# Block-causal attention and a gated unit: a written instruction order replaced by another, with staging rings of five instead of six and the last output tile in two halves

## The chip, the cores and the metric

The kernel runs on one core of a Trainium2 chip. The metric is the device time of the whole program in microseconds (us), as the median of several runs. All engine names are those of the profile: PE is TensorE (matmuls), PEld its weight loads, DVE is VectorE, ACT is ScalarE, POOL is GpSimd, and SP is SyncE, whose queue issues nearly all the transfers.

## The reference

Attention with a block mask (a query sees its own block of 64 keys and all before it), then a gated unit whose gate is a causal convolution of five taps:

```python
B, H, S, D = 8, 8, 576, 64
scores = q @ k.T / sqrt(D)
scores = where(block(i) >= block(j), scores, -1e9)      # block = position // 64
attn = softmax(scores)
x = (attn @ v).transpose(0, 2, 1, 3).reshape(B, S, 512)  # heads side by side

gate_pre = sum(conv_w[k] * x_shifted_by(4 - k) for k in range(5))
gate = sigmoid(gate_pre)
out = (gate * (x @ w_val)) @ w_out                       # float32, [8, 576, 512]
```

The inputs are float32; q, k and v are drawn at a tenth of a normal draw.

## The kernel before, in words

**Order.** Nothing is scheduled by a compiler. The whole program is one long string of *words* (`PLAN`, line 20 on), and `run` executes them one by one: each word calls a function that issues the instructions of one step. Each engine works off its own instructions strictly in the order in which the words stand, so the string fixes the order on every engine and in SP's queue of transfers at once. A word carries numbers and, behind an `@`, either the PSUM banks that it writes (`@45`: banks 4 and 5; there are eight) or the engine that does it (`@A` ACT, `@D` DVE, `@P` POOL).

**Attention.** A "couple" a = 0 to 15 is four heads' worth of q or k, 576 rows of 64. For it `Lqk.a.0` and `Lqk.a.1` load q and k (576 KB each) into the ring `qks`; `cq` casts each to fp16; `tq` transposes it on DVE; `kz` copies the two end blocks of k into a small padded tile. `s.a.t...` computes the transposed scores of key tiles t = 0, 1, 2. The array's four strips of 32 rows work on four heads at once: rows 0 and 1 are half r = 0, rows 2 and 3 are half r = 1. A word such as `s.0.0.0.0.2.1@0123` computes two halves side by side (couple 0, t = 0, r = 0 and couple 0, t = 2, r = 1), `s.2.0@2367` both halves of one t, and a word with three numbers, such as `s.3.2.0@01`, one half alone. `e.a.t.r` takes the exponential of one half on ACT, reading its two banks and writing `pt`. There are 96 of them. `m.p` masks the pair p = 2a + r on POOL (a copy and two memsets). `Lv.p`, `cv.p`, `Lvt`, `cvt` load v (two transfers of 128 KB each) and cast it on POOL with a column of ones. `av.p.h` multiplies probabilities and v for one head (15 small matmuls), `n.p.h` normalises on DVE (a reciprocal and a multiplication), then `xtr.p` transposes on PE and `xt.p` evacuates on DVE, or `xd.p` does both by a transposing transfer in SP's queue (10 of the 32 pairs).

**Gated unit.** When a batch of four pairs stands in `xt`, `cn.n` runs the convolution (80 matmuls of 32 x 32 tiles, into four banks), `th.n.r` takes the tanh on ACT, `val.n.x` projects with `w_val` (four matmuls), `gv.n.x` multiplies the two on DVE, `o.n.t` projects with `w_out` (four matmuls), `oc.n.t` evacuates to `osb` and `st.n.t` stores. n = 0 to 7 are the batches' first 512 rows; n = 8 and 9 collect the last 64 rows of four batches each. `DG` on POOL builds the taps' diagonal tiles, which `cn.0` is the first to need; `wv`, `wo`, `wp`, `wq` prepare the weights.

**Fillers.** `w@b` is one 128 x 128 x 512 matmul on zeros into bank b; nothing reads it. There are 19 of them.

**Rings.** The line `NQS, NVS, ... = 6, 6, 3, 2, 4, 7, 4, 3, 2, 5` sets how many staging buffers q/k (`qks`), v (`vst`) and the rest have. A load into a ring waits until the cast of what lay there is done, and whatever stands behind it in SP's queue waits too. `osb` has five buffers for the output tiles, which take turns in the order of `TILES`.

**The first couple.** `START` and the words `cqr`, `tqr` bring in k and q of couple 0 in parts: k in two parts of 10 and 8 of its 18 column groups, q in three of 4, 6 and 8, each part cast in two pieces by ACT, DVE and POOL.

**The end.** Batch 7's last row tile is written in two halves of 256 columns (`o.7.3`, `o.7.4`); tile `o.9.1` is the last one of all and is written whole. `store` sends a tile of n = 8 or 9 as two transfers of 64 rows.

Of the kernel before, what the change touches and what calls it, by code (L numbers as in the profile page):

```python
# [15 lines left out]
w@0 w@0 Lqk.1.0 w@0 Lqk.1.1 w@0 w@0 Lqk.2.1 w@0 Lcn w@0 Lvt.0 w@0 w@0 Lv.0 cqr.1.1.0@A cqr.1.0.1@D  # L16
cqr.1.1.1@P cqr.1.0.0@A tqr.1.1 tqr.1.0 cqr.0.1.0@A cqr.0.2.1@P cqr.0.2.0@D cqr.0.0.0@P kz.0@A
cqr.0.1.1@P tqr.0.2 cqr.0.0.1@P tqr.0.0 tqr.0.1 s.0.0.0.0.2.1@0123 Lqk.2.0 cq.1.0@P
s.0.2.0.0.1.1@4567 e.0.0.0 tq.1.0 Lv.1 cq.1.1@P e.0.1.1 w@0 w@0 e.0.2.0 w@0 tq.1.1 cq.2.1@P
s.0.0.1.0.1.0@0167 e.0.2.1 Lqk.3.0 kz.1@D Lv.3 s.1.2.0@45 e.0.1.0 cvt.0 tq.2.1 cv.0 w@2 e.1.2.0 cw@2  # L20
m.0 kz.2@D e.0.0.1 Lqk.3.1 s.1.0@6745 cq.2.0@P cT Lv.2 av.0.0@2 e.1.0.0 av.0.1@3 n.0.0 cv.1
s.1.1.0@01 e.1.0.1 s.1.1.1@67 n.0.1 m.1 tq.2.0 e.1.1.1 s.1.2.1@23 Lwv.1 cq.3.0@P Lv.5 av.1.1@4
e.1.2.1 av.1.0@5 n.1.1 xtr.0@6 cv.3 e.1.1.0 s.2.0.1@23 xt.0 m.3 n.1.0 s.2.1.1@67 e.2.0.1 s.2.1.0@01
tq.3.0 Lvt.1 m.2 s.2.2.1@45 e.2.1.1 Lwv.0 av.3.0@2 cq.3.1@P Lv.4 av.3.1@3 e.2.2.1 s.2.0.0@67 n.3.1
cv.2 e.2.1.0 n.3.0 s.2.2.0@45 m.5 av.2.1@3 tq.3.1 Lqk.4.0 e.2.2.0 av.2.0@2 Lqk.4.1 DG@P n.2.1
e.2.0.0 Lv.6 s.3.2.0@01 kz.3@D xtr.1@3 n.2.0 e.3.2.0 cvt.1 s.3.0.0.3.1.1@4567 xt.1 cv.5 xtr.3@2
e.3.1.1 s.3.2.1@01 m.4 Lwo.1 xt.3 wv.2@D av.5.0@3 Lwo.0 e.3.0.0 av.5.1@2 cv.4 Lv.7 n.5.0 w@6 e.3.2.1
s.3.1.0.3.0.1@6745 wv.3@D xtr.2@3 n.5.1 e.3.0.1 cq.4.0@P w@0 av.4.0@0 xt.2 xtr.5@1 wv.1@A wv.0@D
cn.0@4523 e.3.1.0 Lqk.5.0 xt.5 cq.4.1@P tq.4.0 Lqk.5.1 av.4.1@1 th.0.0 Lvt.2 val.0.2@6 n.4.0 m.6
th.0.1 tq.4.1 val.0.3@0 cv.6 Lv.8 wo.1@A gv.0.2 kz.4@P s.4.1.1.4.2.0@4523 n.4.1 av.6.0@6 e.4.1.1  # L30
wo.0@P gv.0.3 val.0.0@7 n.6.0 e.4.2.0 m.7 Lqk.6.1 wp@1045 val.0.1@6 wq.2@A wq.0@D cv.7 wq.3@A gv.0.0
av.6.1@2 wq.1@A Lv.9 av.7.0@3 gv.0.1 cq.5.0@P s.4.1.0.4.0.1@0145 n.6.1 n.7.0 av.7.1@6 e.4.0.1
o.0.0@7 cq.5.1@P n.7.1 Lqk.6.0 e.4.1.0 tq.5.0 s.4.2.1.4.0.0@2345 Lv.11 cvt.2 o.0.2@6 e.4.0.0
oc.0.0@D cv.8 xtr.4@0 tq.5.1 e.4.2.1 xtr.6@1 m.8 o.0.3@7 Lqk.7.1 xt.4 m.9 s.5.2.0.5.1.1@4523 xt.6
oc.0.3@D av.8.0@0 e.5.2.0 kz.5@P o.0.1@1 oc.0.2@D cv.9 e.5.1.1 n.8.0 cq.6.1@P st.0.2
s.5.1.0.5.0.1@6745 oc.0.1@D Lv.10 av.9.0@0 e.5.0.1 xtr.7@1 cq.6.0@P n.9.0 w@2 Lqk.7.0 s.5.2.1@23
e.5.1.0 s.5.0.0@45 xt.7 Lv.13 tq.6.1 cv.11 av.9.1@0 e.5.2.1 w@1 av.8.1@1 tq.6.0 Lqk.8.1 e.5.0.0
cn.1@2367 m.11 n.8.1 cq.7.1@P Lqk.9.0 n.9.1 val.1.2@4 th.1.0 Lqk.8.0 kz.6@D val.1.3@5 m.10 th.1.1
tq.7.1 s.6.1.0.6.2.1@0123 cv.10 st.0.0 gv.1.3 val.1.1@6 e.6.1.0 Lvt.3 kz.7@P gv.1.2 cq.7.0@P
Lqk.10.1 av.10.0@7 e.6.2.1 gv.1.1 s.6.1.1.6.2.0@4501 Lv.14 n.10.0 xtr.9@6 e.6.2.0 xt.9 av.11.0@2  # L40
av.11.1@3 tq.7.0 e.6.1.1 w@0 s.6.0.0@67 n.11.0 s.7.0@0145 Lqk.9.1 e.6.0.0 n.11.1 av.10.1@2 e.7.0.0
xtr.8@3 m.12 xtr.11@6 xt.8 val.1.0@7 Lv.12 e.7.0.1 n.10.1 cq.8.1@P xt.11 s.7.1.0@01 s.6.0.1@23
gv.1.0 s.7.2.0@45 e.7.1.0 cq.8.0@P xtr.10@6 o.1.3@7 xt.10 e.6.0.1 tq.8.1 val.2.0@6 cv.13 Lqk.11.0
e.7.2.0 m.13 oc.1.3@D Lv.15 s.7.2.1@01 tq.8.0 cn.2@4523 cvt.3 e.7.2.1 cq.9.0@P s.8.2.1@01 th.2.0
Lvt.5 o.1.1@7 Lqk.10.0 m.14 kz.8@A gv.2.0 th.2.1 Lv.16 val.2.1@4 oc.1.1@D cq.9.1@P e.8.2.1 av.13.1@5
gv.2.1 s.8.2.0.8.0.1@2367 n.13.1 cv.12 o.1.0@0 e.8.0.1 st.0.1 cv.14 st.1.1 s.7.1.1@45 cv.15 e.8.2.0
s.8.1.0@67 Lvt.4 tq.9.0 val.2.2@1 st.0.3 e.7.1.1 av.12.1@2 tq.9.1 e.8.1.0 Lv.17 val.2.3@3 m.15
n.12.1 oc.1.0@A s.8.0.0.8.1.1@4567 cq.10.1@P Lqk.11.1 kz.9@A gv.2.3 av.12.0@0 e.8.0.0 Lv.19 gv.2.2
av.13.0@2 cq.10.0@P n.12.0 av.14.1@3 e.8.1.1 av.14.0@1 n.13.0 w@0 cq.11.0@P n.14.0
s.9.1.1.9.2.0@4567 xtr.12@2 n.14.1 e.9.2.0 av.15.1@0 xt.12 m.17 av.15.0@1 n.15.1 e.9.1.1  # L50
s.9.0.1.9.1.0@2367 m.16 n.15.0 o.1.2@0 e.9.0.1 tq.10.1 cvt.4 xtr.14@1 e.9.1.0 xtr.13@4 cv.16 o.2.2@5
# [36 lines left out]
"""


@with_exitstack
def kernel(
    ctx: ExitStack,
    tc: tile.TileContext,
# [8 lines left out]
    nc = tc.nc  # L103
# [5 lines left out]
    B, H, SEQ, D = q.shape  # L109
# [389 lines left out]
```

## Time and profile before

| | |
|---|---|
| runs | 171.86 us (median of three: 171.4, 171.86, 173.29) |
| the profiled execution | 170.84 us, of which the span from the first to the last instruction is 169.1 us |
| PE, PEld | busy 158.1 and 99.8 us, 3117 instructions each |
| ACT | busy 128.5 us; the 96 exponentials take 92.1 us of it |
| DVE | busy 124.0 us |
| POOL | busy 100.5 us; 30 full casts of q or k take 42.0 us |
| transfers | 41.97 MB, 248 GB/s on average |

A busy PE in this table says that a matmul was in flight, not that the array did as much as it can: matmuls overlap, and their ends are modelled. To see how full PE is, the starts of consecutive matmuls are compared. The "chain" of a profile is the work that ended last, followed back from the end: at each step to what released it, or to the instruction before it on its engine.

### The profile page before, as it was taken

How to read it: one execution, taken by the hardware profiler on the slowest of the kernel's cores; microseconds unless marked ns; L12 is line 12 of the kernel's file. 1: busy time of each engine (PE TensorE's matmuls, PEld its weight loads, DVE VectorE, ACT ScalarE, POOL GpSimd, SP SyncE). 2: the span in 40 equal slices, each digit the busy share in tenths (PEclk: the TensorE clock that was granted, in tenths of full speed). 3: DMA queues.
4: the chain of work that ended last, by engine and by line, in shares of the span. 5: the costliest groups of instructions: out<-in, count | busy, mean ns of one | idle time of the engine just before them, and what ended most of it. 6: DMA issues, size and time to landing. Idle time of an engine off the chain costs nothing.

```text
span 169.1 us, 7342 instructions
## 1 busy us (share of the span) xinstructions
PE 158.1 (94%) x3117; PEld 99.8 (59%) x3117; DVE 124.0 (73%) x264; ACT 128.5 (76%) x158; POOL 100.5 (59%) x193
## 2 busy tenths in 40 slices
PE   7299989899999999999999999999999999999980
PEld 2047776646675865577665676665647568454640
DVE  3775988999999976699897489568897638542640
ACT  5479999798797998998858898978578983537230
POOL 5688999959688299789495449454993424000000
PEclk9999999999999999999999999999999999999996
DMA  5999979999569999993589499999989687853665
GB/s 191 400 357 355 312 203 342 364 363 325 184 153 309 372 359 276 317 294 98 145 214 373 117 289 172 238 357 161 357 237 254 131 152 107 174 189 124 224 217 125
DMA packets 55867, 41.97 MB, mean 248 GB/s; under 512 B 45973, under 2 KB 46229, under 8 KB 55834
## 3 DMA queue, kind: packets, MB, share of 16 engines
q1 hardware_dynamic: 55690, 41.37, 85.2%
q8 instruction: 24, 0.39, 1.0%
q10 hardware_dynamic: 144, 0.13, 0.2%
q14 instruction: 9, 0.07, 0.1%
HBM read 30.42 MB, written 9.44 MB: 236 GB/s over the span
## 4 chain that ended last, share of the span: by engine, by line
PE 81%; ACT 6%; DVE 6%; DMA 2%; issue 1%; POOL 0%; DVEq 0%
PE B L113 78%; ACT pt L279 6%; PE B L316 4%; DMA qks<-in_k_dram 2%; DVE kT L240 2%; DVE qT L240 2%; DVE x L309 1%; DVE rc L308 0%; ACT w_val L230 0%; POOL qk L224 0%; ACT osb L224 0%; DVE xt L329 0%; DVE qk L224 0%; DVEq L308 0%; DVEq L240 0%
## 5 line engine op out<-in xcount | busy, mean ns | idle before, releaser
L279 ACT ACTIVATE pt<-B 128x1024 f16<-128x1024 f32 x96 | 92.1, 1034 | 13.8 <-PE B L113 13.1
L224 POOL CAST qk<-qks 128x1152 f16<-128x1152 f32 (+2 forms) x35 | 43.8, 1268 | 14.8 <-DMA qks<-in_k_dram 6.1
L113 PE MATMUL B<-qT,kT 32*128 32x448 f16 (+3 forms) x640 | 35.1, 296 | 4.0 <-DVE qT L240 3.2
L113 PEld LDWEIGHTS <-pt 128*128 128x128 f16 x960 | 33.1, 98 | 5.9 <-issue 1.1
L113 PE MATMUL B<-xt,w_val 128*128 128x512 f16 (+1 forms) x160 | 36.0, 359 | 0.0
L113 PE MATMUL B<-w_out,gv 128*128 128x512 f16 (+1 forms) x148 | 35.8, 374 | 0.0
L113 PE MATMUL B<-v,pt 128*128 128x65 f16 x896 | 35.1, 194 | 0.0
L309 DVE TENSOR_TENSOR x<-B,rc 128x320 f16<-128x320 f32 x64 | 31.5, 492 | 2.3
L385 DVE SCALAR_TENSOR_TENSOR gv<-th,B 128x512 f16<-128x512 f32 (+1 forms) x40 | 24.1, 628 | 12.3 <-ACT th L373 8.9
L113 PEld LDWEIGHTS <-kT 32*128 32x128 f16 x640 | 19.0, 95 | 20.8 <-issue 11.8
L373 ACT ACTIVATE th<-B 128x1024 f32<-128x1024 f32 (+1 forms) x20 | 18.1, 939 | 10.6 <-PE B L113 10.6
L113 PEld LDWEIGHTS <-w_val 128*128 128x128 f16 x160 | 14.0, 98 | 12.5 <-issue 1.1
L218 POOL CAST v<-vst 128x512 f16<-128x512 f32 x32 | 19.5, 618 | 3.2 <-PE B L113 1.9
L240 DVE STREAM_TRANSPOSE qT<-qk 128x576 f32<-128x576 f32 (+3 forms) x18 | 19.4, 1107 | 2.4 <-PE B L113 1.6
L308 DVE RECIPROCAL rc<-B 128x5 f32<-128x5 f32 x64 | 11.8, 185 | 11.7 <-PE B L113 11.6
L240 DVE STREAM_TRANSPOSE kT<-qk 128x576 f32<-128x576 f32 (+2 forms) x17 | 19.5, 1153 | 1.3 <-POOL qk L224 0.7
L287 POOL MEMSET pt<- 64x384 f16 x32 | 13.2, 412 | 11.1 <-ACT pt L279 9.7
L113 PEld LDWEIGHTS <-gv 128*128 128x128 f16 x148 | 13.0, 98 | 11.5 <-issue 0.6
L224 ACT COPY osb<-B 128x512 f32<-128x512 f32 (+1 forms) x21 | 11.8, 582 | 9.1 <-PE B L113 4.8
L286 POOL COPY pt<-pt 128x128 f16<-128x128 f16 x32 | 9.6, 300 | 8.7 <-ACT pt L279 8.3
L113 PE MATMUL B<-xt,DG 32*32 32x512 f16 (+1 forms) x800 | 13.3, 357 | 0.1
L113 PE MATMUL B<-v16t,pt 128*128 128x65 f16 x64 | 12.4, 194 | 0.0
(46 smaller groups left out, 109.3 us busy)
## 6 DMA issues: line engine op xcount, KB each, us to landing
qks<-in_k_dram SPq DMA_DIRECT2D x16, 576.0 KB, 6.6
qks<-in_q_dram SPq DMA_DIRECT2D x16, 576.0 KB, 5.3
vst<-in_v_dram SPq DMA_DIRECT2D x64, 128.0 KB, 5.2
out_dram<-osb SPq DMA_DIRECT2D x31, 256.0 KB, 3.4
out_dram<-osb SPq DMA_DIRECT2D x9, 128.0 KB, 2.8
vtst<-in_v_dram SPq DMA_DIRECT2D x8, 128.0 KB, 6.6
th<-in_moe_w_val_dram SPq DMA_DIRECT2D x2, 512.0 KB, 7.1
osb<-in_moe_w_out_dram SPq DMA_DIRECT2D x2, 512.0 KB, 7.1
```

The source lines that it names most:

```text
L113: nc.tensor.matmul(out=out, lhsT=lhsT, rhs=rhs, start=start, stop=stop, skip_group_check=True)
L218: nc.gpsimd.tensor_copy(out=v16s[p % NV][0:128, 0:4, 0:2, 0:64], in_=vst[p % NVS][0:128])
L224: (eng.copy if eng is nc.scalar else eng.tensor_copy)(out=o, in_=i)
L240: nc.vector.transpose(out=(qT, kT)[i][a % NQT][0:128].bitcast(fp32).rearrange("p c (x n) -> p c n x", n=9)[:, :, x // 2:y // 2], in_=qk16[ ...
L279: nc.scalar.activation(out=pts[(2 * a + r) % NPT][0:128, 0:2, 512 * t:512 * t + 512], in_=two(bank["s", a, t, 2 * r], bank["s", a, t, 2 * ...
L286: nc.gpsimd.tensor_copy(out=pt[0:128, 0:2, 1536:1600], in_=pt[0:128, 0:2, 0:64])
L287: nc.gpsimd.memset(pt[64:128, 0:2, 0:1536].rearrange("p h (t s) -> p h t s", t=3)[:, :, :, 0:64], 0.0)
L308: nc.vector.reciprocal(out=rc[0:128], in_=O[:, :, 64:65])
L309: nc.vector.tensor_tensor(out=x16[p % NX16][0:128, 0:5, h, 0:64], in0=O[:, :, 0:64], in1=rc[0:128].to_broadcast([128, 5, 64]), op=ALU.mult)
L316: nc.tensor.transpose(out=f16(m[0])[:, 128 * i:128 * i + 128], in_=x16[p % NX16][0:128, i, 0:2, 0:64], identity=ident16[0:128, 0:128])
L373: nc.scalar.activation(out=ths[ORDER.index(n) % NTH][0:128, 2 * r:2 * r + 2, 0:w], in_=two(bank["cn", n, 2 * r], bank["cn", n, 2 * r + 1], w),
L385: nc.vector.scalar_tensor_tensor(out=gvs[z % NG][0:128, x, 0:w], in0=ths[z % NTH][0:128, x, 0:w], scalar=1.0, in1=f32(bank["val", n, x])[: ...
```

## The change

The string `PLAN` is replaced as a whole: 832 words before, 833 after. The same steps are in it, with the same 19 fillers and the same 10 transposing transfers; their order, their banks and, for some, their engine differ. Beside that, `NQS` and `NVS` go from 6 to 5, and the last tile of n = 9 is written in two halves: `o.9.1` and `o.9.2` instead of `o.9.1`, the second of the halves' two transfers on ACT's queue.

By count of words: scores as 59 words instead of 61 (halves that stand alone: 22 instead of 26); 38 `o`, `st` instead of 37; `cq.1.0` on DVE, all other full casts on POOL as before; `kz` on ACT, DVE, POOL 2, 6, 8 times instead of 6, 4, 6; `oc` 24 times on ACT and 14 on DVE instead of 21 and 16; of the casts of the first couple four on ACT, two on DVE, four on POOL instead of 3, 2, 5; `wv` 2 on ACT, 2 on DVE instead of 1 and 3. Of the fillers six stand ahead of the first scores instead of nine, nine (instead of six) between them and `cn.0`, and four behind it in both.

```diff
 PLAN = """
-w@0 w@0 Lqk.1.0 w@0 Lqk.1.1 w@0 w@0 Lqk.2.1 w@0 Lcn w@0 Lvt.0 w@0 w@0 Lv.0 cqr.1.1.0@A cqr.1.0.1@D
-cqr.1.1.1@P cqr.1.0.0@A tqr.1.1 tqr.1.0 cqr.0.1.0@A cqr.0.2.1@P cqr.0.2.0@D cqr.0.0.0@P kz.0@A
-cqr.0.1.1@P tqr.0.2 cqr.0.0.1@P tqr.0.0 tqr.0.1 s.0.0.0.0.2.1@0123 Lqk.2.0 cq.1.0@P
-s.0.2.0.0.1.1@4567 e.0.0.0 tq.1.0 Lv.1 cq.1.1@P e.0.1.1 w@0 w@0 e.0.2.0 w@0 tq.1.1 cq.2.1@P
-s.0.0.1.0.1.0@0167 e.0.2.1 Lqk.3.0 kz.1@D Lv.3 s.1.2.0@45 e.0.1.0 cvt.0 tq.2.1 cv.0 w@2 e.1.2.0 cw@2
...
+w@0 w@0 Lqk.1.0 w@0 Lqk.1.1 w@0 w@0 Lv.1 w@0 Lcn Lvt.0 cqr.1.1.1@A cqr.1.0.0@D cqr.1.1.0@P
+cqr.1.0.1@A tqr.1.1 Lqk.2.0 tqr.1.0 Lv.2 cqr.0.1.0@A cqr.0.2.1@P cqr.0.1.1@D cqr.0.0.1@A cqr.0.2.0@P
+tqr.0.1 cqr.0.0.0@P tqr.0.2 kz.0@P tqr.0.0 s.0.0.0.0.2.1@0123 cq.1.0@D s.0.0.1@45 e.0.0.0 s.0.1.1@67
+e.0.2.1 cq.1.1@P tq.1.0 s.0.2.0@01 Lqk.2.1 e.0.0.1 Lv.0 s.0.1.0@23 tq.1.1 e.0.1.1 cvt.0 w@4 w@4
+kz.1@D e.0.2.0 m.1 s.1.2.1.1.1.0@4567 Lqk.3.0 e.0.1.0 cv.1 Lqk.3.1 w@0 w@0 cq.2.0@P Lv.3 e.1.2.1
+s.1.2.0.1.1.1@0123 e.1.1.0 m.0 tq.2.0 w@4 e.1.2.0 av.1.0@4 cq.2.1@P Lqk.4.1 w@5 e.1.1.1 Lvt.1 n.1.0
+s.1.0@0167 cv.0 cw@5 tq.2.1 e.1.0.1 cv.2 w@4 Lv.5 e.1.0.0 cq.3.0@P av.0.1@4 kz.2@D cT s.2.0@2367
+n.0.1 s.2.1.1@01 e.2.0.1 m.2 tq.3.0 av.0.0@4 w@5 Lwv.0 e.2.1.1 av.1.1@5 cq.3.1@P n.0.0 Lqk.4.0
+s.2.1.0@67 n.1.1 e.2.0.0 av.2.1@0 cv.3 xtr.0@1 e.2.1.0 m.3 s.2.2@4523 xt.0 Lwv.1 tq.3.1 xtr.1@1 Lv.6
+e.2.2.0 cq.4.1@P av.3.0@6 n.2.1 av.3.1@7 e.2.2.1 Lv.4 s.3.1.0@45 xt.1 kz.3@P n.3.0 cvt.1 e.3.1.0
+s.3.2@0123 n.3.1 cv.5 av.2.0@6 e.3.2.1 m.5 xtr.3@7 n.2.0 s.3.0.1@45 e.3.2.0 tq.4.1 DG@P av.5.0@6
+Lwo.1 s.3.0.0@23 e.3.0.1 xt.3 s.3.1.1@01 n.5.0 cq.4.0@P w@7 e.3.0.0 xtr.2@7 Lwo.0 av.5.1@6 xt.2
+Lqk.5.1 wv.0@A wv.3@D m.4 cn.0@2345 Lqk.5.0 wv.2@A wv.1@D Lv.7 e.3.1.1 cv.6 n.5.1 val.0.3@7 th.0.0
+tq.4.0 Lqk.6.0 m.7 val.0.0@6 th.0.1 cv.4 s.4.1.0@01 gv.0.0 Lvt.2 m.6 av.4.0@2 e.4.1.0 kz.4@D xtr.5@3
...
+o.8.0@3 kz.15@P oc.4.2@D s.14.1.0.15.1.1@6745 oc.8.0@A n.27.0 st.4.2 val.5.2@1 e.14.1.0 xd.24
+av.25.0@0 st.4.1 e.15.1.1 gv.5.2 m.28 s.15.0.0.15.2.1@2367 av.25.1@1 e.15.0.0 cv.26 o.5.3@4 n.25.1
+cv.29 Lv.31 e.15.2.1 n.25.0 o.5.1@5 cvt.7 xd.25 s.14.2.1.15.2.0@2301 oc.5.1@D st.8.1 av.28.1@6
...
+val.9.2@1 val.9.3@2 gv.9.0 st.7.2 gv.9.2 o.7.3@3 gv.9.3 o.7.4@0 oc.7.3@A o.9.1@1 oc.7.4@D st.7.3
+o.9.0@2 oc.9.1@D st.7.4 st.9.1 o.9.2@3 oc.9.0@A oc.9.2@A st.9.0 st.9.2
 """
...
-    NQS, NVS, NQ16, NQT, NV, NPT, NX16, NG, NTH, NO = 6, 6, 3, 2, 4, 7, 4, 3, 2, 5
+    NQS, NVS, NQ16, NQT, NV, NPT, NX16, NG, NTH, NO = 5, 5, 3, 2, 4, 7, 4, 3, 2, 5
...
-    TILES = [(n, t) for n in ORDER for t in range({7: 5, 8: 2, 9: 2}.get(n, 4))]
+    TILES = [(n, t) for n in ORDER for t in range({7: 5, 8: 2, 9: 3}.get(n, 4))]
...
+    def row(n, t):
+        return min(t, {7: 3, 9: 1}.get(n, t))
...
-        c, i = cols(n, t), 128 * min(t, 3)
+        c, i = cols(n, t), 128 * row(n, t)
...
-            s = n - 8 + 2 * t + h
-            nc.sync.dma_start(
+            s = n - 8 + 2 * row(n, t) + h
+            (nc.scalar if (n, t, h) == (9, 2, 1) else nc.sync).dma_start(
                 out=out[s if n == 8 else 8 - s, 512:SEQ, c], in_=o[64 * h:64 * h + 64, c])
...
-        return slice(256 * (t - 3), 256 * (t - 2)) if n == B - 1 and t > 2 else slice(0, 512)
+        z = t - {7: 3, 9: 1}.get(n, 9)
+        return slice(256 * z, 256 * z + 256) if z >= 0 else slice(0, 512)
```

## The prediction

> **What bounds the kernel now.** I read the windows first, then the chain, then the timeline.
>
> ```profile
> 16.00:24.00 8.00, 7.68 (x175) 5.89 (x171) 6.41 (x15) 8.00 (x10) 7.62 (x16) 1.00 1.03 303
> 24.00:32.00 8.00, 7.09 (x171) 5.26 (x185) 7.33 (x17) 8.00 (x10) 7.61 (x12) 1.00 0.93 306
> 36.00:100.00 64.00, 63.91 (x1359) 41.22 (x1354) 54.17 (x112) 54.97 (x65) 47.27 (x81) 1.00 0.85 256
> 100.00:164.40 64.40, 64.35 (x1218) 39.66 (x1210) 42.77 (x91) 43.28 (x56) 24.56 (x53) 1.00 0.84 207
> ```
>
> Columns: stretch, length, then busy time of PE, PEld, DVE, ACT, POOL, granted clock, DMA share, GB/s. From 16 to 32 us ACT is full (8.00 of 8.00) and POOL nearly; from 36 us on only PE is. The chain says the same:
>
> ```profile
> 9.56 5.62 ACT pt L279 x6
> ...
> 25.35 0.61 PE B L113 x8
> ...
> 34.33 1.14 DVE kT L240
> 35.47 0.05 issue
> 35.52 7.95 PE B L113 x138
> ...
> 146.25 18.11 PE B L113 x244
> 164.36 0.02 issue
> 164.38 0.58 ACT osb L224
> ```
>
> A busy PE need not be a full one, so I look at the starts of its matmuls:
>
> ```profile
> 1.20 4.02 PE L113 MATMUL B<-wz 128*128 128x512 f16 x9 [1.20 <-DVE tiny L451]
> ...
> 142.79 1.35 PE L113 MATMUL B<-xt,DG 32*32 32x512 f16 x80
> 144.07 1.90 PE L113 MATMUL B<-xt,w_val 128*128 128x512 f16 x8
> 145.81 0.44 PE L316 MATMUL B<-ident,x 128*128 128x128 f16 x5
> ```
>
> Between starts: a projection of four matmuls takes 1.74/2 = 0.87 us, a convolution 144.07-142.79 = 1.28. Likewise an `av` takes 0.46, an `xtr` 0.28, a pair of score halves 0.55 to 0.61. A half alone takes as much (25.35 above: 8 matmuls, 0.61), unless another half on the other strips follows; then 0.33 on average. A full-width word ahead of scores or a convolution takes 0.09 more.
>
> **The part that PE bounds.** With these prices the old words from `cn.0` (start 31.80) to the last matmul sum to 132.4 us; the trace took 164.36-31.80 = 132.6. So there are 0.2 us of stalls in 132: nothing to win there except by fewer or cheaper words. The new string's sum: `av` 31.5 (before 30.9), convolutions 12.7 (12.7), output projections 32.1 (32.2), scores 31.5 (32.0; four lone halves fewer), `val` 32.1 (32.3), `xtr` 6.7, fillers 4.7, weights 0.4 in both. Total 151.7 against 151.9, because the changes of width (54 instead of 51), more of them behind `av`, give back most of what the lone halves and the `val` words save. But 18.7 of it stand before `cn.0`, where 19.5 stood: 133.1 us are left after it, 0.7 more than before. Taking the same 0.2 of stalls, PE ends 133.3 us after `cn.0` starts. The question is when that is.
>
> **The start, new order.** Same transfers first: k lands at 4.8, q at 6.2, as POOL's and ACT's first casts show. The pieces of q now cost POOL 0.45+0.4+0.35 instead of 0.45 and three of 0.35, ACT takes one more: q's last transposition ends near 8.1, not 8.33. First scores 8.1 (before 8.38), first exponential 9.3 (9.56). ACT's exponentials step by 0.905, so the fourth ends at 9.3+2.7+1.0 = 13.0. The cast `cq.1.0` on DVE (256 columns took 0.28 to 0.31, so some 1.2 for 1152) ends at 9.4, before k of couple 1 is cast (that one waits for its transfer until 9.1, as before), so it hides there; without that cover it would cost its 1.2.
>
> POOL is then idle from 11.0 until 13.0, because `m.1` needs the fourth exponential. Behind it stand, up to `DG`, five masks (0.96 each), five casts of q or k (1.35), five of v (0.56), a tail (0.67), a `kz` (0.40), `DG` (1.3): 16.7 us, so `m.5` ends at 28.4, `DG` at 29.7. `av.5.0`, `s.3.0.0` follow `m.5` on PE and end at 29.6; that exponential is the 23rd and in ACT's own pace would start at 9.3+22x0.905 = 29.2.
>
> One wait is added. `kz.2` is now on DVE, dispatched about 0.2 us after POOL begins `cq.3.0`. What that does, the trace shows:
>
> ```profile
> 11.08 1.40 POOL L224 CAST qk<-qks 128x1152 f16<-128x1152 f32 x1 [0.47 <-DMA qks<-in_k_dram]
> ...
> 11.89 0.67 DVE L224 COPY kz<-kT 128x256 f16<-128x256 f16 x1
> ...
> 25.75 0.28 DVE L224 COPY kz<-kT 128x256 f16<-128x256 f16 x1
> ```
>
> The copy took 0.67 and ended 0.08 after POOL's cast. [...] So `kz.2` ends near 20.8 instead of 19.9. Behind it on DVE wait `n.0.1` and `tq.3.0`; PE waits in `s.2.0`, ACT for the 13th exponential, 21.1 instead of 20.2. The last price is smaller: the 23rd starts at 21.1+9.05 = 30.1 instead of POOL's 29.6. [...]
>
> `cn.0` at 31.3 (31.0 to 31.9), against 31.80. After it DVE's `wv.3`, `wv.1`, `n.5.1`, `tq.4.0` end near 34.3 and PE reaches `s.4.1.0` at 34.3: no wait, and no cover to spare. PE ends at 31.3+133.3 = 164.6 (before 164.4).
>
> **The end.** After PE's end 4.7 us pass, of which SP's queue of four 64-row transfers (some 0.55 each, the last issued at 166.4) sets the end. In the new order the half tile's two go 0.8 earlier, three stand behind, one is on ACT: the last issue is some 0.3 earlier (from 0 to 0.6).
>
> **Fillers, rings, other moves.** The six fillers before the first scores wait on nothing and cost nothing; the nine later ones are in the sum above and lie in ACT's part, where PE has some 3 us to spare. Five staging buffers: the moved loads lead their casts by 4.6 us of PE work at least in the dense part (5.0 before); v landed after 2.4 to 9.1, median 5.2. The tightest is `Lv.31`, below. The rest of the shuffled `kz` and `oc` work leaves DVE, ACT and POOL under PE in each 10 us of the dense part bar one (DVE 11.1, where before it had 10.3 and stalled nobody).
>
> **Sum against the profiled execution.** 169.1 + 0.2 - 0.3 = 169.0 of span, 170.8 with the 1.7 around it. The median of the runs is 1.0 above that execution and the runs spread over 1.9, so something differs from run to run. In this one the first fillers take 4.02/9 = 0.43 us each, twice the 0.22 of later, and matmuls quicken near 12.9 us; the granted clock reads 1.00 there all the same. [...] Had the change come 3 us later, the old order's lone half, taps and `s.1.0` around 13 to 16 us would each take double, and ACT, unbroken in this trace, would wait some 0.7; the new order holds two score words and fillers ahead of ACT there and would lose some 0.1. I take that difference whole, since the median lies 1.0 above the profiled execution: 171.86 - 0.05 - 0.6 = 171.2.
>
> **Rivals.** (1) Forecast, a tie within 1% (170.1 to 173.6; nearer than that, measurements of this kernel do not tell): 0.6, own range 170.2 to 172.6. Chain for it: PE's sum.
> [...] 0.2 for over 1%.
> (3) Slower: the ring of five. `Lv.31` waits for `cv.26`, 32.1 us of PE work before the end; before, it was issued 40.4 before it. Its two transfers (issue 1.0, landing some 3 in that stretch, 5.2 at the median) let `cv.31` run at 27 to 25.3; masks and `cv.30` queue behind it on POOL and must be done when `av.31.1` and `av.30.0` are due at 23.2 and 22.3. It decides from a landing over 5.2; at the slowest 9.1 it costs 3.9 plus nothing gained: 175; I take 2.5: 173.7. Stores and transposing transfers ahead of it in SP's queue (waits up to 7 us there) speak for it. 0.2, with the gate below.
> (4) The clock: PE is idle from 3.8 to 8.1 now, 3.2 us before. If it quickens only after about 19.7, PE's spare 3.4 us are spent and each later us costs 0.5: 24 gives +2.1, 173.3. [...] In (3)'s 0.2.
>
> **Numbers.** 171.2; the range 169.7 to 173.5 takes in (2)'s end and (3)'s usual price and leaves 2 in 10 outside. Faster by over 1%: 0.2; within: 0.6; slower: 0.2.
>
> **What would show it.** Right: `cn.0` near 31.3, PE full from there, 133 us to its end, `kz.2` over 0.6 long, the last issue near 2 us after PE's end. Wrong: a gap on PE after 36 us (then which ring or bank), or `cn.0` after 32.

## The result, and the profile after

| | before | after |
|---|---|---|
| all runs of the comparison | 173.18 us (170.84 to 175.03, 20 runs) | 173.3 us (172.5 to 174.97, 20 runs) |
| the profiled execution, its span | 170.84, 169.1 | 173.37, 171.6 |
| words of PE end at | 164.4 | 166.4 |
| from there to the end of the span | 4.7 | 5.2 |

The ratio is 1.0114, with a 95% interval of 1.0085 to 1.0144. It leaves out runs more than 1.5% above the fastest of the same kernel, which cuts the long runs of the kernel before and none of the new one's, so it compares the fast ends; the medians of all runs differ by 0.1 us. Both are true, and the study is about how they go together. The forecast was 171.2, which is 0.66 under the 171.86 that stood for the kernel before; the lower bound of the ratio excludes a gain.

The windows of the kernel after; columns as in the prediction (PE, PEld, DVE, ACT, POOL, clock, DMA share, GB/s):

```profile
16.00:24.00 8.00, 8.00 (x168) 5.71 (x164) 6.72 (x13) 7.47 (x9) 7.61 (x13) 0.89 1.05 335
24.00:32.00 8.00, 7.86 (x197) 5.79 (x197) 7.18 (x17) 8.00 (x10) 7.60 (x14) 1.00 0.97 288
36.00:100.00 64.00, 63.66 (x1369) 42.40 (x1367) 55.98 (x113) 54.38 (x64) 46.07 (x78) 1.00 0.84 251
100.00:164.40 64.40, 63.95 (x1213) 38.98 (x1212) 41.34 (x92) 43.79 (x55) 25.34 (x55) 1.00 0.87 209
```

PE is as busy as before from 36 us on, but for 0.25 and 0.4 us. They lie in two places, which its chain of waits shows (start, length, what):

```profile
34.92 0.69 DVE gv L383
35.60 0.97 DVE kz L222
36.57 0.60 DVE gv L383
37.18 0.04 issue
37.22 5.85 PE B L111 x97
...
146.09 0.89 SPq L321
...
148.34 0.54 SPq L406
...
149.92 4.75 DMA out_dram<-osb
...
154.76 0.69 DVE osb L222
155.45 0.60 DVE gv L383
156.05 0.04 issue
156.10 9.89 PE B L111 x132
```

In the kernel before, PE stood in the chain without a break from 146.25 to its end. Here, from `cn.0` on, the chain leaves PE twice. PE's own timeline has a wait at both places (start, length, engine, line, operation, and behind it the wait and what ended it):

```profile
36.57 0.30 PE L111 MATMUL B<-qT,kT 32*128 32x320 f16 x1
37.22 0.59 PE L111 MATMUL B<-qT,kT 32*128 32x320 f16 x11 [0.34 <-DVE gv L383]
37.62 0.28 PE L111 MATMUL B<-qT,kz 32*128 32x64 f16 x8
37.85 0.59 PE L111 MATMUL B<-v,pt 128*128 128x65 f16 x14
...
154.61 1.03 PE L111 MATMUL B<-w_out,gv 128*128 128x512 f16 x4
156.10 1.02 PE L111 MATMUL B<-xt,w_val 128*128 128x512 f16 x4 [0.46 <-DVE gv L383]
```

The first time DVE's `kz.4` holds `gv.0.3`, whose bank the next scores write. The timelines of POOL and DVE at that place say why:

```profile
35.45 1.04 POOL L222 CAST w_out<-osb 128x1024 f16<-128x1024 f32 x1
...
35.52 1.05 DVE L222 COPY kz<-kT 128x256 f16<-128x256 f16 x1
36.49 0.67 DVE L383 SCALAR_TENSOR_TENSOR gv<-th,B 128x512 f16<-128x512 f32 x1
```

The shortest copy of this kind took 0.22 us in this trace. Beginning 0.07 after POOL's `wo.0`, it took 1.05 and ended 0.08 after it: the same wait that the prediction priced for `kz.2`, at a second place. The scores, which cost 0.61, took 1.28 from their first matmul to the next word (36.57 to 37.85), 0.67 too much.

The second time `gv.7.0` stands on DVE behind `oc.6.2`, and that behind the landing of `st.5.1`, whose buffer it writes. The store had gone out at 149.92, behind the transposing transfer `xd.31` and other stores in SP's queue. `val.7.1` starts 1.49 after the word ahead of it, where 0.87 is the price of that word: 0.62 late.

### The profile page after: what moved, and what is told of

It reads as the page before. It is cut to its first block, busy times and chain, and to the rows that moved or that the text cites. A ratio compares the mean times of both kernels' runs of the same rounds, so it can differ in the third digit from the quotient of the medians.

```text
span 171.6 us, 7363 instructions
## 1 busy us (share of the span) xinstructions
PE 160.2 (93%) x3121; PEld 101.4 (59%) x3121; DVE 124.4 (72%) x264; ACT 129.1 (75%) x159; POOL 99.5 (58%) x193
## 4 chain that ended last, share of the span: by engine, by line
PE 82%; DMA 6%; DVE 5%; SPq 2%; issue 2%; ACT 1%; DVEq 0%
PE B L111 78%; PE B L314 3%; DMA qks<-in_q_dram 3%; DMA out_dram<-osb 3%; DVE gv L383 1%; SPq L406 1%; DVE kT L238 1%; SPq L410 1%; DVE x L307 1%; DVE kz L222 1%; DVE xt L327 1%; DVE qT L238 1%; SPq L321 1%; DVE rc L306 0%; DVE osb L222 0%
## 5 line engine op out<-in xcount | busy, mean ns | idle before, releaser
L222 POOL CAST qk<-qks 128x1152 f16<-128x1152 f32 (+2 forms) x33 | 42.2, 1285 | 10.1 <-DMA qks<-in_k_dram 3.6
L111 PE MATMUL B<-qT,kT 32*128 32x448 f16 (+3 forms) x640 | 36.6, 303 | 4.5 <-DVE qT L238 4.1
L111 PEld LDWEIGHTS <-pt 128*128 128x128 f16 x960 | 34.0, 98 | 6.4 <-issue 1.4
L111 PE MATMUL B<-v,pt 128*128 128x65 f16 x896 | 36.1, 194 | 0.0
L307 DVE TENSOR_TENSOR x<-B,rc 128x320 f16<-128x320 f32 x64 | 31.5, 491 | 2.3
L222 ACT COPY osb<-B 128x512 f32<-128x512 f32 (+1 forms) x24 | 13.4, 572 | 13.2 <-PE B L111 10.1
L238 DVE STREAM_TRANSPOSE qT<-qk 128x576 f32<-128x576 f32 (+3 forms) x18 | 19.7, 1105 | 3.9 <-POOL qk L222 3.0
L216 POOL CAST v<-vst 128x512 f16<-128x512 f32 x32 | 19.7, 620 | 3.8 <-DMA vst<-in_v_dram 2.7
L222 DVE COPY osb<-B 128x512 f32<-128x512 f32 (+1 forms) x14 | 9.1, 649 | 7.1 <-DMA out_dram<-osb 4.4
```

The lines of the kernel that those rows point to most:

```text
L111: nc.tensor.matmul(out=out, lhsT=lhsT, rhs=rhs, start=start, stop=stop, skip_group_check=True)
L216: nc.gpsimd.tensor_copy(out=v16s[p % NV][0:128, 0:4, 0:2, 0:64], in_=vst[p % NVS][0:128])
L222: (eng.copy if eng is nc.scalar else eng.tensor_copy)(out=o, in_=i)
L238: nc.vector.transpose(out=(qT, kT)[i][a % NQT][0:128].bitcast(fp32).rearrange("p c (x n) -> p c n x", n=9)[:, :, x // 2:y // 2], in_=qk16[ ...
L307: nc.vector.tensor_tensor(out=x16[p % NX16][0:128, 0:5, h, 0:64], in0=O[:, :, 0:64], in1=rc[0:128].to_broadcast([128, 5, 64]), op=ALU.mult)
```

## The experiments

Three theories. **A:** the new order has lasting stops of its own (the two above and five 64-row stores on SP's queue at the end). **B**, the forecast's own step: the moment at which the clock rises decides a run's time. **C**, formed after the first four runs: both kernels lose time in stops that fall anew in each run. Runs 1 to 4 set A against B, the later ones A against C. With each group of runs the kernel before was timed too, on the same chip. Those runs and the 20 above, 146 together: median 172.98, fastest tenth under 171.2, 170.1 to 177.2.

**1. The kernel before once more,** unedited.

> The kernel before, unchanged, for a second trace and for the granted clock of each run. Its 20 runs spread from 170.84 to 175.03 us, the new kernel's from 172.5 to 174.97. Theory A (waits that the new order adds on PE and in SP's queue make the 1.1%): the spread of before has nothing to do with it, and a second trace of before shows PE without gaps from 36 us on, whatever its time. Theory B (the moment at which the clock rises makes it): runs of before with a granted clock near 0.97 (half clock for some 10 us at the start, as in the trace of the new kernel) take 173 to 175 us, runs with 0.99 or more take 171.

Measured: 173.02 (170.29 to 175.22), ratio 1.0003 [0.9934, 1.0072]. Its trace has the clock rise at 13.72 us (12.89 in the first) and gives 171.94. Mean granted clock does not sort the runs: the shortest had 0.978, two at 1.0 took 171.94 and 172.69, and one at 0.98 took 172.32. So B falls as it was put. A small share of the clock remains: of the 138 runs of the kernel before that have a clock on record, those under 0.985 have a median 0.5 us above the others, in a spread of 7 us. The new kernel's 32 runs show 0.4 in the same way, so it does not tell the two orders apart. The 171.86 of three runs that the forecast started from was low: the median is about 173.0, and the profiled 170.84 is among the 9 shortest of 146.

**2. The kernel before without its nine first fillers.**

```diff
-w@0 w@0 Lqk.1.0 w@0 Lqk.1.1 w@0 w@0 Lqk.2.1 w@0 Lcn w@0 Lvt.0 w@0 w@0 Lv.0
+Lqk.1.0 Lqk.1.1 Lqk.2.1 Lcn Lvt.0 Lv.0
```

> The old order without the nine fillers ahead of the first scores (nothing reads them). Theory B: without them PE has done nothing before 8.4 us, so the clock can't rise early and fall back; every run is like the trace of before, 170.8 to 171.6 us, median under 171.6, spread under 1 us, ratio to before 0.99 over all runs. Theory A, or that the fillers do warm PE for the first scores: no change of the spread, or all runs later, 172 to 173.5.

Measured: 173.96 (173.43 to 175.9), ratio 1.0135 [1.0071, 1.0199]. In its trace, the longest of the six runs, the clock rose at 21.44. The fillers are worth about 1 us (172.92 with them on that chip). B's shorter time didn't come; of its small spread there is a trace, since five of the six runs lie within 0.7 us.

**3 and 4. Each stop taken away alone:** `kz.4` on POOL; `st.5.1` ahead of `xd.26`.

```diff
-e.4.1.0 kz.4@D xtr.5@3
+e.4.1.0 kz.4@P xtr.5@3
```

```diff
-n.29.0 xd.26 e.15.1.0
+n.29.0 st.5.1 xd.26 e.15.1.0
...
-st.5.3 val.6.3@0 gv.6.1 st.5.1 xt.30
+st.5.3 val.6.3@0 gv.6.1 xt.30
```

> The new order with kz.4 on POOL instead of DVE, ahead of wo.0 on POOL. In the trace of the new kernel kz.4 on DVE took 1.05 us (35.52 to 36.57), until POOL's wo.0 was done, gv.0.3 stood behind it, and PE stood 0.67 us in s.4.2.0.4.0.1. Theory A: that wait falls to under 0.1 and the time by 0.5 to 0.7 us (ratio to before 0.3 to 0.4% lower than the new kernel's 1.011). Theory B: no change beyond 0.2 us, because DVE or the bank of e.4.1.0 ends the wait at the same time.

> The new order with the one store st.5.1 moved ahead of the transposing transfers xd.26 to xd.31 in SP's queue. In the trace of the new kernel it landed at 154.67, held oc.6.2 on DVE until 154.76 and with it gv.7.0, and PE stood 0.6 us in val.7.1. Theory A: that wait goes, PE has no gap there, 0.4 to 0.6 us less (ratio to before 0.3% lower than the new kernel's). Rival: the store st.4.3, which lands at 155.28 and holds oc.6.0 on ACT, ends the same wait next, and less than 0.2 us is won.

Measured: 173.28, ratio 1.0072 [1.0025, 1.0119], and 173.37, ratio 1.0064 [1.0025, 1.0104]. Each ratio is 0.4 to 0.5% under 1.0114, as A has it. But the intervals overlap, the medians hardly differ from the unedited new kernel's (173.3), and that kernel, timed again in run 5, gave 1.0041, lower than either. So the times do not show what one edit alone is worth; the traces show that its stop is gone. PE's timeline in the run with the earlier store:

```profile
153.28 1.03 PE L111 MATMUL B<-w_out,gv 128*128 128x512 f16 x4
154.14 1.03 PE L111 MATMUL B<-xt,w_val 128*128 128x512 f16 x4
155.01 1.03 PE L111 MATMUL B<-w_out,gv 128*128 128x512 f16 x4
155.87 1.03 PE L111 MATMUL B<-xt,w_val 128*128 128x512 f16 x4
156.73 1.46 PE L111 MATMUL B<-w_out,gv 128*128 128x512 f16 x6
```

Words at 0.86 to 0.87 each: that stop is gone. In the run with `kz.4` on POOL (the profiled one was long, 175.16) the 0.67 is gone too, but something else is there:

```profile
31.67 1.26 PE L111 MATMUL B<-xt,DG 32*32 32x512 f16 x62
33.96 0.60 PE L111 MATMUL B<-xt,DG 32*32 32x512 f16 x18 [1.03 <-issue]
```

PE stops after 62 of the 80 matmuls of `cn.0`, which wait for nothing that the others don't. "issue" means that the profile knows no releaser. This is where theory C begins. The transfers' records have 24 "instruction" packets of 16,384 bytes. Counted by the number of the matmul, such stops of the first traces stand here:

```
kernel                  matmul no. (mod 128)   gap us   after a packet's landing, us
before, again (1)       478 (94)               0.86     1.37
                        2140 (92)              1.02     1.41
no first fillers (2)    1757 (93)              0.65     1.35
                        2140 (92)              0.67     1.38
                        2396 (92)              1.74     1.39
kz.4 on POOL (3)        479 (95)               1.40     1.36
```

The stops recur at the same place modulo 128, so by this count a packet holds 128 matmuls with their weight loads, 256 instructions, or 64 bytes for each (16,384/256). They stand where a packet's content ends, and PE starts 1.35 to 1.41 us after the next has landed. Over the traces of the whole study there are 25 such stops of PE of over 0.15 us, and in each the packet that had landed last, 1.2 to 1.6 us earlier, is by this count the one with the next matmul in it. From the crossing of one border (worked out by the count) to the start of the next packet it took about 0.5 us when the DMA engines moved little and up to 6.5 when they were full; over 192 packets of eight traces this time goes with the data moved in between (correlation 0.95).

**5 to 8, together: the new kernel again; its last tile whole; six buffers; three edits together.**

```diff
-    TILES = [(n, t) for n in ORDER for t in range({7: 5, 8: 2, 9: 3}.get(n, 4))]
+    TILES = [(n, t) for n in ORDER for t in range({7: 5, 8: 2, 9: 2}.get(n, 4))]
...
-o.9.0@2 oc.9.1@D st.7.4 st.9.1 o.9.2@3 oc.9.0@A oc.9.2@A st.9.0 st.9.2
+o.9.0@2 st.7.4 o.9.1@3 oc.9.0@A st.9.0 oc.9.1@A st.9.1
```

```diff
-    NQS, NVS, NQ16, NQT, NV, NPT, NX16, NG, NTH, NO = 5, 5, 3, 2, 4, 7, 4, 3, 2, 5
+    NQS, NVS, NQ16, NQT, NV, NPT, NX16, NG, NTH, NO = 6, 6, 3, 2, 4, 7, 4, 3, 2, 5
```

> The changed kernel itself once more, unedited, timed beside the kernel before on one chip. Theory A (the new order has lasting stops of its own: kz.4 behind wo.0, 0.67 us; val.7.1 behind the store st.5.1, 0.62; the five 64-row stores of the end, 0.8; sum 2.1 us or 1.2%): median of all runs 1.0 to 1.3% above that of the kernel before on this chip, about 174.7 where the kernel before shows 172.9, and the same stops in the profile, each within 0.2 us. Theory C (both kernels lose 1 to 4 us a run in stops that fall anew each time: PE resumes about 1.37 us after a packet of its own instructions has landed, and those packets start late when the DMA engines are full; the three lasting stops take the place of such losses rather than adding to them): median of all runs within 0.4% of the kernel before, and in the profile at least one stop on PE put down to issue, starting again 1.3 to 1.45 us after an instruction packet landed, which the first profile of the changed kernel did not have.

> The changed kernel with its last tile whole again (ten stores of the end as four 128-row and no 64-row ones; ORDER's tile 9 in two pieces instead of three). Theory A: PE's end to span's end 4.6 to 4.8 us instead of 5.2, two lone halves with o and val less on PE (another 0.3), so 0.5 to 0.8 us or 0.3 to 0.5% below the unedited changed kernel of the same call. Theory C: the profile's tail is shorter by the same 0.4 to 0.8 us (the tail is no random stop), but the median moves by less than 0.2%. My forecast of the prediction (split is 0.3 us cheaper): 0.2% above the unedited one.

> The changed kernel with six staging buffers for q and k and six for v instead of five. Rival 3 of the prediction (a ring of five makes loads wait for their buffer, Lv.31 first of all): 0.5 us or more below the unedited changed kernel of the same call, loads issued earlier and PE's stops at val and av gone. Theory A and Theory C: within 0.2% of the unedited one, every load issued at the same place of SP's queue within 0.3 us, since the place in SP's queue and not the buffer held them.

> The changed kernel with kz.4 on GpSimd, the store st.5.1 ahead of xd.26, and the last tile whole: the three lasting stops taken away together. Theory A: they add up, 1.9 us or 1.1% below the unedited changed kernel of the same call, ratio to the kernel before 0.996 to 1.003. Theory C: the three stops are gone from the profile, but less than half of their sum shows in the median of all runs (0.1 to 0.5% below the unedited one), and stops on PE that end 1.3 to 1.45 us after an instruction packet landed still stand in the profile.

Measured, with the kernel before at 173.18 (170.1 to 177.2):

- New kernel again: 173.61 (172.54 to 175.21), ratio 1.0041 [1.0005, 1.0077]. Both lasting stops on PE are in its trace, as A has it, but A's 1.0 to 1.3% above in the median did not come (0.25%); C's stop on PE was not there. The same two kernels gave 1.0114 in the first comparison, and the two intervals do not meet: this ratio moves with the draw of the runs by more than its interval says.
- Last tile whole: 173.66, no gain, against A, and no shorter tail, which both theories expected. The trace explains it: from the last matmul's start to the end 5.3 us, where the split tile shows 5.0 in four of six traces and 5.4 and 5.5 in two. In those two, DVE's copy of the first of the 64-row tiles waits 0.31 and 0.47 for the landing of the store whose buffer it takes; in the other four it does not wait. So the longer tail was no lasting loss, and the first profile showed a bad draw.
- Six buffers: 183.73, and not a test of the ring, whose share of the time stays unmeasured. With six, q of couple 11 and v of pair 27 are loaded, by the written order, into buffers whose old content (q of couple 8, v of pair 21) is not yet cast, so those two are computed from wrong data, and POOL's casts wait for the later load (one such wait is 9.6 us). A written order belongs to its ring sizes.
- Three edits: 172.88 (171.69 to 175.92), ratio 0.9977 [0.9941, 1.0013]: 0.42% under the unedited one, within C's 0.1 to 0.5%, far from A's 1.1%, though A's ratio of 0.996 to 1.003 to the kernel before holds. Its trace has again 1.40 us of "issue" after 62 matmuls of `cn.0`.

**9. One more load** of 768 KB ahead of `Lwo.0`, into a buffer that nobody reads.

> The changed kernel with one more load of 768 KB (three quarters of w_out into a spare buffer that nobody reads) on SP's queue just ahead of Lwo.0, about 28 us. Theory C (PE's own instructions come in packets over the same DMA engines, and PE stops when one starts late): the instruction packet asked for near 27.6 us starts about 2 us later than without the load, at 30.5 us or later, and PE stops in the middle of the independent matmuls of cn.0, from about 32.5 us, for 1.5 to 3.5 us, put down to issue, starting again 1.3 to 1.45 us after that packet has landed; the first profile of the changed kernel has no stop there. Theory A, or data alone: no stop inside cn.0; what is late is a wait for a load (cq.5.1 or wo.0 on POOL, by up to 2 us), shown as such, after 35 us.

Measured: 172.83 (one run), no stop in `cn.0`. The packet started at 29.0 and not at 30.5, though the load had gone out at 27.99. C's step fails here: a packet isn't simply queued behind every load issued before it.

**10 and 11. Both kernels with half of each load of q, k and v left out** from about 20 us on (so the attention is computed from stale halves; 31.5 instead of 42 MB are moved).

```diff
-        nc.sync.dma_start(out=qks[(2 * a + i) % NQS][0:128], in_=src)
+        n = slice(0, 9 if a > 3 else 18)
+        nc.sync.dma_start(out=qks[(2 * a + i) % NQS][0:128, n], in_=src[:, n])
...
-                out=vst[p % NVS][0:128, 0:4, h, 0:64],
-                in_=v[b, 2 * g + h, 0:512, 0:64].rearrange("(c p) d -> p c d", p=128))
+                out=vst[p % NVS][0:128, 0:2 if p > 5 else 4, h, 0:64],
+                in_=v[b, 2 * g + h, 0:256 if p > 5 else 512, 0:64].rearrange("(c p) d -> p c d", p=128))
```

> The kernel before with half of each load of q, k and v left out from about 20 us on (the loads' number and places in SP's queue stay; the output is computed from stale halves). Theory C: with the DMA engines less full the stops that fall anew each time are gone: median within 0.7 us of the lowest time that the kernel before ever showed (170.1), so 169.4 to 170.8, and lowest to highest under 3 us where it was 7.1. Theory A, or PE alone as the bound: the median stays above 172.2, with the same spread.

> The changed kernel with the same halves of the loads left out. Theory A and C together (the lasting stops cost their 1.5 to 2.1 us when nothing else stops PE, and hide in the kernel's own random stops when the DMA engines are full): 1.3 to 2.1 us above the kernel before with half loads, 0.8 to 1.2% where the full kernels differ by 0.25%. If the new order has no lasting loss: within 0.5 us of it.

Measured: the kernel before 171.18 (170.32 to 172.58), ratio 0.9912 [0.9874, 0.995]: 1.4 under its full loads on that chip (172.56) and with half of their spread there (2.3 us in 12 runs against 4.4 in 29); the median misses the expected 170.8 by 0.4. The new order 173.83 (172.73 to 174.77), ratio 1.0069 [1.0031, 1.0108], no shorter than with full loads. The gap of the medians is 2.65 us, 1.5%, more than the 1.3 to 2.1 expected. But the new order's twelve runs stand in two groups of six, 172.73 to 173.28 and 174.37 to 174.77, so no run lies near their median; the one group is about 1.8 above the kernel before, the other 3.3. So part of what the kernel before loses from run to run depends on how full the DMA engines are; the new order's loss does not go with it.

The only trace of the new order here (172.97, of the lower group) shows the stop behind `st.5.1` and one of 0.9 us inside `cn.0`, 1.47 after a packet's landing. The stop behind `kz.4` is not there, though nothing in the edit bears on it. POOL and DVE:

```profile
35.39 1.04 POOL L223 CAST w_out<-osb 128x1024 f16<-128x1024 f32 x1
...
36.34 0.22 DVE L223 COPY kz<-kT 128x256 f16<-128x256 f16 x1
```

The stop in `cn.0` made everything behind it late, `kz.4` came when `wo.0` was nearly over, and nothing waited. So here a late packet took a lasting stop's place. It does not always: with the whole last tile (run 6) both stops stand in the trace. What makes the upper group of six, no trace shows.

**12 and 13. Four edits:** the three, and `Lwo.0` behind `Lv.7`, `wo.0` behind `cq.5.1`; then the same again.

```diff
-xtr.2@7 Lwo.0 av.5.1@6 xt.2
+xtr.2@7 av.5.1@6 xt.2
...
-wv.1@D Lv.7 e.3.1.1
+wv.1@D Lv.7 Lwo.0 e.3.1.1
...
-n.4.0 wo.0@P s.4.2.0.4.0.1@6701
+n.4.0 s.4.2.0.4.0.1@6701
...
-cq.5.1@P wp@4301
+cq.5.1@P wo.0@P wp@4301
```

> The changed kernel with kz.4 on GpSimd, st.5.1 ahead of xd.26, the last tile whole, and Lwo.0 behind Lv.7 on SP's queue, three loads later (wo.0 behind cq.5.1 on GpSimd, so that it doesn't hold that one). Theory C: the instruction packet asked for near 27.7 us starts by 29.5 us, no stop inside cn.0, and the median is 0.3 to 0.8 us under the 172.88 of the three edits, 172.1 to 172.6, ratio to the kernel before 0.993 to 0.998. Theory A: the three edits took all that there is, 172.7 to 173.1; if wo.0 now comes late, wp waits for it and it is slower.

> The kernel of the four edits once more, as the unshifted comparison of this call. Theory C: its runs fall in two groups some 1.4 us apart, as the last ones did (seven from 171.6 to 172.3, four from 173.5 to 174.4), the longer ones with a stop inside cn.0 where an instruction packet came late; median 172.0 to 172.6. Theory A: one group, no stop inside cn.0.

Measured: 172.2 (before on that chip 172.56), ratio 1.0027 [0.9982, 1.0071]; again: 173.69 (before 173.06), ratio 1.0053 [1.0008, 1.0098]. The expected gain did not hold, nor did two clear groups, and the stop in `cn.0` was there in the second's trace (1.1 us of "issue").

**14 to 16. The packets' borders moved against the work:** tiny matmuls among the first fillers, where PE idles, 12 and 60 in the four edits, 76 in the kernel before.

```diff
-w@0 w@0 Lqk.1.0 w@0 Lqk.1.1 w@0 w@0 Lv.1 w@0 Lcn Lvt.0
+w@0 w@0 Lqk.1.0 w@0 Lqk.1.1 w@0 w@0 Lv.1 w@0 Lcn z.60@0 Lvt.0
...
+    def tiny_mm(n, m):
+        for i in range(n):
+            mm(f32(m[0])[0:32, 0:8], wz[0:32, 0:32], wz[0:32, 0:8])
```

> The same kernel with 12 tiny 32x32 matmuls of 8 columns among the first fillers, where PE idles 4.1 us ahead of the first scores: no work added to the path, but every later instruction stands 12 matmuls further on in the packets of 256 instructions (128 matmuls with their weight loads). Theory C: PE has 4.7 us instead of 4.2 for the 128 matmuls of the shortest stretch, from 27.5 us; worked out from the waits of the first six profiles of this family, the stops fall from 1.3 us a run to 0.2, so the longer group is gone or rare and the median 0.4 to 1.0 us below the unshifted kernel of this call. Theory A, or any cause in the data: the same as the unshifted within 0.3 us.

> The same kernel with 60 such tiny matmuls (about 2.5 us of the 4.1 idle ones). Theory C: the worst place for the packets, short stretches of 4.5 to 5 us where the DMA engines are fullest (31.5, 51, 91 us): the same working gives 3.3 us of stops a run instead of 1.3, so 1 to 2.5 us above the unshifted kernel of this call, with stops put down to issue that end 1.3 to 1.45 us after a packet landed, at places other than the middle of cn.0's first words. Theory A, or data: the same as the unshifted within 0.3 us.

> The kernel before with 76 such tiny matmuls ahead of its first scores (about 3 us of the 3.2 idle ones; up to 0.5 us of delay of the first scores, if they take longer, is to be taken off). Theory C: 4.9 us of stops a run by the same working instead of 1.6 (29.4, 48.7, 90.6 us), so 1.5 to 3.5 us above the kernel before. Theory A, or data: within 0.5 us of it.

Measured: 12 gave 173.85 (ratio 1.0004), 60 gave 175.74 (1.0235), beside 173.69 without (1.0053); 76 gave 177.01 in six runs (172.43 to 178.73), beside 173.06. So the medians rose by 2.05 and 3.95 us for matmuls that run in idle time: first scores started at 8.06 and 8.22 in their traces, not late. PE's timeline of the kernel before with 76, in the one of its shorter runs that was profiled (173.93):

```profile
32.80 0.56 PE L113 MATMUL B<-v,pt 128*128 128x65 f16 x13
36.10 0.20 PE L113 MATMUL B<-v,pt 128*128 128x65 f16 x1 [2.73 <-issue]
...
42.82 0.55 PE L113 MATMUL B<-v,pt 128*128 128x65 f16 x12
43.67 0.22 PE L113 MATMUL B<-v,pt 128*128 128x65 f16 x2 [0.30 <-issue]
```

The stops are now inside an `av`, at matmuls 606 and 733: 94 and 93 modulo 128, the same places in the packets, at other work, 1.50 and 1.41 us after a packet landed. That settles that these stops belong to the stream of instructions and not to data. In this trace "issue" sums to 3.6 us; the runs near 178 have no trace. For the 60 the trace shows only 0.8 us of "issue", and 0.9 on a transposing transfer; its 2.05 is not all explained. The 12 took the stop in `cn.0` away, as worked out, but the time did not fall; there `wp` waited 1.1 us for `wo.0`, which the fourth edit had made late.

**17 and 18. The three edits without and with the 12,** `Lwo.0` at its old place.

> The kernel of the three edits (kz.4 on GpSimd, st.5.1 ahead of xd.26, the last tile whole; Lwo.0 at its old place) once more, as the comparison of this call. Theories A and C alike: as before, a median within 0.5% of the kernel before of this call, 172.5 to 173.5; and a stop inside cn.0 in about half of the runs.

> The same with the 12 tiny matmuls in PE's idle time at the start, Lwo.0 at its old place, so that wo.0 on GpSimd isn't late for wp as it was in the four edits with 12 (1.1 us). Theory C: no stop inside cn.0, 0.4 to 1.0 us below the unshifted kernel of this call, 0.2 to 0.8% under the kernel before. If the packets matter only where they are made worse (60 and 76 tiny matmuls), or random late data fills the place of the stop: the same as the unshifted within 0.3 us.

Measured: 172.61 (ratio 1.0075 [0.9983, 1.0166]) and 172.79 (1.0081 [0.9997, 1.0165]), with the kernel before at 174.19 in 11 runs. No stop at a border with the 12; without, three of 0.55 to 0.58 (matmuls 990, 1245, 1756: 94, 93 and 92 modulo 128). Still no gain of time. That the borders can be placed worse is shown; that they can be placed better is not.

No version beats the kernel before for certain. All runs of the three edits together: median 172.78 (19 runs) against 172.98; its fastest is 171.69, and 27 of the 146 runs of the kernel before were shorter. Against the unedited new order (173.42, 32 runs) the three edits together are 0.64 us shorter; drawing the runs anew, with repetition, puts this between 0.2 and 1.35 in 95 of 100 draws. So the lasting stops do cost time, but less than the 1.9 us that A added up.

## Why the prediction was wrong, step by step

- **First scores and `cn.0`: right,** and by the steps that were named: first scores at 8.05 for 8.1, the 13th exponential at 20.96 for 21.1, `DG` done at 29.79 for 29.7, `cn.0` at 31.48 for 31.3, within its 31.0 to 31.9. `kz.2` went as priced, from 19.48 to 20.54, 0.08 past the end of POOL's cast (19.05 to 20.46). How much of the 31.3, and of its range, is the price of this wait was the author's estimate, and no run shows it, since none moves `kz.2`; the trace shows the copy itself, 1.06 where the shortest took 0.22. The 0.28 that the prediction showed as the free copy was itself held a little: POOL's `DG` ran until 25.95 there, and the copy ended 0.08 later.

```profile
18.24 1.21 DVE L238 STREAM_TRANSPOSE kT<-qk 128x576 f32<-128x576 f32 x1
19.48 1.06 DVE L222 COPY kz<-kT 128x256 f16<-128x256 f16 x1
```

- **"Taking the same 0.2 of stalls": this step failed.** 133.3 us were forecast from `cn.0` to PE's end; it took 134.9. The sum of the words was right to 0.3: of the 1.6 too much, 0.67 is `kz.4` behind `wo.0` and 0.62 the store; the rest, 0.3, is not placed. The forecast had such a wait in hand for `kz.2` (0.67 in the trace before, ended 0.08 after POOL's cast) and didn't look for one at the other `kz`; it said of this very stretch that there was "no cover to spare". For `oc` it compared sums of busy time per 10 us, which say nothing of a copy that stands in front of a multiplication and waits for a buffer. Runs 3 and 4 removed one each. A gap on PE after 36 us was the prediction's own sign of being wrong, and both gaps are that.
- **The end "0.3 shorter": off.** From the last matmul's start, 5.1 before and 5.0 to 5.5 after: from 0.1 shorter to 0.4 longer, by whether the first 64-row tile has to wait for its buffer. The fifth store on SP's queue was counted, this wait was not.
- **171.86 + ... - 0.6, from execution to median: failed.** The gain of 0.6, the term that put the forecast under the kernel before, was laid on the moment of the clock, which was to cost the old order 0.7 and the new one 0.1. Both figures were the author's estimate, and no run shows them. The runs with a clock on record show nothing of that difference: those with a lower mean clock are 0.5 longer in the old order and 0.4 in the new one. And the median that it started from was 1.1 too low. Before `cn.0` the clock did little in the new order, as forecast: with rises from 14.9 to 17.8 `cn.0` started between 31.4 and 31.7 in every trace of it but that of the one run of 523.61 us.
- **Luck.** 173.3 lies inside the stated 169.7 to 173.5, and the medians of the first comparison are a tie as forecast. The lower end was the author's estimate, and no run of the new order came near it: the shortest of its 32 unedited runs took 172.5. The upper end of that range was paid for by the ring of five, which did not come; what filled it was the two waits and the low starting median.
- **Rivals.** Rival 3's ring of five was not it: the new kernel's trace has no wait of PE for v or for a load, and `Lv.31` held nobody. Rival 4 needed a rise after 19.7; no trace of the new order records one. The first trace comes nearest: PE worked from 8.05 on, and the clock stayed at half until 17.83. Slower came, by a mechanism that neither rival had: two waits on DVE, each for something in another engine's queue (0.67 and 0.62 us of PE).
- **Why the median hardly moved for all that: open in part.** Over all runs (32 of the one, 146 of the other) the medians differ by 0.44 us. The short runs differ by more (lowest tenth under 172.6 and 171.2), the long ones not at all (upper tenth above 174.6 and 174.9). Halving the loads takes 1.4 us off the old order's median and nothing off the new one's. That the lasting stops and the late packets take each other's place, so that they do not add up, fits all this; run 11's trace shows one such case and run 6's the opposite, so as the cause of the small difference it is argued and not shown.

## What to carry to other kernels

When an order is rewritten, sums of busy time are not enough: go through each instruction of the second-busiest engine and ask what it waits for, on a cast that POOL has under way (0.67 us of PE here) or on a store that still reads the buffer (0.62), and who is queued behind it. Before forecasting 1% on a kernel whose runs spread by 3%, find out where in that spread the profiled execution lies. And where a profile says "issue" in the middle of like instructions, count them: here 25 stops ended 1.2 to 1.6 us after a packet of the stream itself had landed, and those listed stood at matmuls 92 to 95 modulo 128.

## What the runs showed of the hardware

- By the count of the stops, PE's code comes in packets of 256 instructions; the new kernel's first trace has 24 of them, 0.39 MB, which take 0.9% of the time of the 16 DMA engines; the data's queue takes 85.0% of the same engines. At 25 stops PE went on 1.2 to 1.6 us after one had landed; the longest stop is 2.9 us from one matmul's start to the next. 76 harmless matmuls at the start made the median 3.95 us longer (six runs).
- The first traces of the two kernels have ten DVE copies of `kz` (128 x 256 in fp16). Two ran while POOL was idle and took 0.22 us each. Seven began during a POOL instruction, took 0.28 to 1.06 (1.05 and 1.06 beside the two casts named above) and ended 0.08 or 0.09 after it. One, begun 0.06 before a POOL copy ended, took 0.23. What holds the seven no trace names.
- The clock fell back once it had risen: in the new kernel's first trace it was full from 4.18 to 7.59 us, half until 17.83 (10.24 us), then full. PE was busy from 8.05 on, all through that (the column behind POOL is the clock):

```profile
8.38:12.00 3.62, 3.62 (x55) 2.21 (x48) 3.01 (x3) 2.77 (x4) 2.02 (x2) 0.50 1.15 322
12.00:16.00 4.00, 4.00 (x42) 1.77 (x38) 0.93 (x3) 4.00 (x6) 3.05 (x7) 0.50 1.11 392
```

- One run in the study (run 12, four edits) took 523.61 us: PE was busy 99% of its span, and the projections with `w_out` took 1062 ns instead of some 370 each. No other run did so, and what slowed it is not known.
